# Two chunks at a time in a fused linear-attention and feed-forward kernel

## The chip, the cores and the metric

The kernel runs on one core of one Trainium2 chip. The metric is the device time of one execution in microseconds (us), as the median of several runs. The engines are TensorE (PE; PEld is its weight load), VectorE (DVE), ScalarE (ACT), GpSimd (POOL) and SyncE (SP), which here issues almost all DMAs.

## The reference

For 4 batches, 8 heads, 768 time steps and head size 48, a decayed linear attention is computed, and its output goes through a feed-forward block with a softmax-weighted unit and a layer norm:

```python
for t in range(S):
    kt, vt, rt = (k[:, :, t], v[:, :, t], r[:, :, t])
    cur = np.einsum('bhd,bhe->bhde', u[None] * kt, vt)
    y[:, :, t] = np.einsum('bhd,bhde->bhe', rt, state + cur)
    state = w[None, :, :, None] * state + np.einsum('bhd,bhe->bhde', kt, vt)
# x: y as (3072, 384)
h = x @ w_in                                   # (3072, 1024)
e = np.exp(h - h_max)
solu = h * (e / (np.sum(e, axis=-1, keepdims=True) + 1e-09))
ln = (solu - mu) / np.sqrt(var + 1e-06) * g_ln # mu, var over the 1024
out = ln @ w_out                               # (3072, 384)
```

All arithmetic is in float32; the weights arrive as 64-bit words.

## The kernel before

The time axis is cut into 6 chunks of 128 steps, so there are N = 24 units (batch, chunk), ordered chunk by chunk with the four batches next to each other. A first path, `direct_path`, computes everything under the assumption that decays, weights and sums lie in a safe range, and writes a flag `bad`; a general path (not executed in these runs) would follow if the flag were set.

Per unit i these helpers issue the work:

- `load` brings k, r and v of a unit (three DMAs on SP). `decay_k` and `decay_r` (GpSimd, L674 and L681) multiply k and r with decay tables; `weigh` (GpSimd, L687, L688) and `sum_own` (VectorE, L692) form the diagonal of the scores, and `diagonal` (ScalarE, L698, eight instructions) writes it into AT.
- k and r are transposed. For units below FIRST = 9 that is done on TensorE (`turn_r`, `turn_k`, L710 and L718). For later ones `halve_rk` splits the 32-bit words into 16-bit halves (ScalarE L859, VectorE L860), a transposing DMA turns them (SP, L834), and `join_rk` puts the words together again (VectorE, L839).
- `scores` (TensorE, L733) multiplies k and r into a PSUM tile of two banks; VectorE copies the lower triangle into AT (L735).
- `finish` multiplies state and AT with r and v into y_ps (TensorE, L760), copies it into xT (ScalarE, L772), forms the outer product kv_ps (TensorE, L778) and updates the state (VectorE L784, GpSimd L785).
- `ffn_in` is the first matmul (TensorE, L795, into h_ps, the only buffer of two banks) and the exponential with its sum (ScalarE, L798). `unit` is the reciprocal and the product (VectorE, L805, L807) and the centring and squares (ScalarE, L809, L810); `deviation` (GpSimd) makes the scale of the layer norm. `halve_ln` (ScalarE, L845), a transposing DMA and `join_ln` (VectorE, L839) turn the result into lnT.
- `ffn_out` is the second matmul (TensorE, L877, o_ps), its scaled copy (ScalarE, L879) and the store (SP, L880).

The order of every engine's instructions is written out by hand: the loop over i issues helper after helper, and every engine takes its instructions strictly in that order. At stage i the loop works on unit i+3 (decays), i+2 (joins, diagonal), i+1 (scores), i (heads and state), j = i - LA = i - 2 (first matmul) and l = i - LA - LO = i - 7 (second matmul). So TensorE's order of a steady stage is h_ps, o_ps, at, y_ps, kv_ps. PSUM tiles tr_ps, tk_ps, y_ps, kv_ps and o_ps rotate through the four one-bank buffers of psM.

The weights are also checked. Each of the 14 weight pieces is loaded a second time, one at each stage from i = 12 on (L506); at the next stage `check_words` takes magnitudes and their sum (ScalarE, L558) and the least (VectorE, L560). `check_range` at i = 10 checks the decays from a row loaded for it, and `check_sums`, ahead of the last `ffn_out`, joins all checks through a small matmul n_ps into `bad`.

## Time and profile before

| | us |
|---|---|
| Median of 6 runs (354.76 to 355.03) | 355.0 |
| The profiled execution | 354.66 |
| Its span, first to last instruction | 352.8 |
| TensorE busy in the span | 337.0 |
| ScalarE busy | 242.4 |
| VectorE busy | 210.7 |
| GpSimd busy | 176.8 |

The span is the time between the first and the last instruction of the profiled execution; the rest of its time lies around it. A busy share is an average over stages, so what a change is worth is read from the stage that it touches: from the chain of work that ended last, which names at each step what released it, and from the timeline. Matmul records of different array tiles overlap, so the distance between their starts tells more than the duration of one.

### The profile page before, as it was taken

Reading aid. Unit: us, or ns where it says so; the run is one execution under the profiler, and the core shown is the slowest. Engines: PE = TensorE matmul, PEld = TensorE weight load, DVE = VectorE, ACT = ScalarE, POOL = GpSimd, SP = SyncE. Lnnn points to the kernel's source line nnn. Section 1 sums busy time; section 2 is a strip of 40 time slices with the busy share of each in tenths; the row PEclk is TensorE's granted clock in tenths of the full one; section 3 lists DMA queues with packets and bytes.
Section 4 is the critical chain, followed back from the end, with each engine's and each line's share of the span. In section 5 each row is a group of like instructions: output and inputs, shape, how many; then the busy total and the mean of one; then the engine's idle time right before and its main releaser. Section 6 shows DMA issues by size and latency. Waiting matters only on the chain.

```text
span 352.8 us, 8407 instructions
## 1 busy us (share of the span) xinstructions
PE 337.0 (96%) x3427; PEld 203.6 (58%) x3427; DVE 210.7 (60%) x323; ACT 242.4 (69%) x457; POOL 176.8 (50%) x196
## 2 busy tenths in 40 slices
PE   2699999999999999999999999999999999999993
PEld 2475566656566566556566566565565565545563
DVE  7795888786468567665865765765772441323320
ACT  3775888988897668677767778778687464465510
POOL 3889667784865754944945846746730000000000
PEclk9999999999999999999999999999999999999999
DMA  8999996269999768988887978966663523541641
GB/s 170 264 236 232 234 219 84 56 106 157 191 195 158 146 130 154 208 173 168 188 167 170 195 162 177 195 151 119 150 129 62 126 69 59 128 124 46 143 103 36
DMA packets 164878, 52.75 MB, mean 150 GB/s; under 512 B 157917, under 2 KB 161246, under 8 KB 164830
## 3 DMA queue, kind: packets, MB, share of 16 engines
q1 hardware_dynamic: 164686, 51.92, 71.9%
q8 instruction: 29, 0.48, 0.6%
q10 hardware_dynamic: 144, 0.20, 0.2%
q14 instruction: 19, 0.16, 0.1%
HBM read 26.94 MB, written 4.72 MB: 90 GB/s over the span
## 4 chain that ended last, share of the span: by engine, by line
PE 89%; POOL 3%; issue 2%; ACT 2%; DVE 1%; DMA 1%; SPq 0%; POOLq 0%
PE o_ps L877 35%; PE h_ps L795 35%; PE y_ps L760 10%; PE at L733 6%; PE kv_ps L778 2%; ACT AT L698 1%; DMA g_sb<-in_moe_g_ln_dram 1%; PE tk_ps L718 1%; POOL kp L674 1%; POOL rku L687 1%; PE tr_ps L710 0%; POOL vt L581 0%; POOL rku L688 0%; DVE solu L807 0%; POOL w_in_sb L540 0%
## 5 line engine op out<-in xcount | busy, mean ns | idle before, releaser
L795 PE MATMUL h_ps<-w_in_sb,xT 128*128 128x512 f32 x288 | 129.9, 600 | 0.6 <-DVE solu L807 0.5
L877 PE MATMUL o_ps<-w_out_sb,lnT 128*128 128x384 f32 (+1 forms) x400 | 127.3, 473 | 0.0
L877 PEld LDWEIGHTS o_ps<-w_out_sb,lnT 128*128 128x128 f32 x400 | 75.1, 190 | 52.8 <-issue 9.1
L795 PEld LDWEIGHTS h_ps<-w_in_sb,xT 128*128 128x128 f32 x288 | 52.8, 190 | 60.5 <-issue 58.0
L698 ACT ACTIVATE AT<-ident,own 128x128 f32<-128x128 f32 x192 | 58.6, 390 | 6.0 <-DVE own L692 6.0
L785 POOL TENSOR_TENSOR state<-state,pw 64x192 f32<-64x192 f32 x32 | 25.6, 801 | 63.0 <-DVE state L784 61.6
L735 DVE COPY_PREDICATED AT<-later,at 128x1024 f32<-128x1024 uint32 x24 | 31.9, 1328 | 31.4 <-PE at L733 31.4
L845 ACT COPY halves<-solu 128x2048 uint16<-128x2048 uint16 x24 | 45.4, 1893 | 0.0
L839 DVE COPY lnT<-halves 128x2048 uint16<-128x2048 uint16 x24 | 37.5, 1563 | 11.7 <-DMA halves<-halves 11.7
L809 ACT ACTIVATE solu<-solu,st 128x1024 f32<-128x1024 f32 x24 | 27.5, 1148 | 22.6 <-DVE solu L807 22.6
L798 ACT ACTIVATE e<-h_ps 128x1024 f32<-128x1024 f32 x24 | 24.5, 1022 | 18.2 <-PE h_ps L795 18.2
L816 POOL TENSOR_SCALAR st<-st 128x1 f32<-128x1 f32 x24 | 7.1, 294 | 59.2 <-ACT e L810 59.2
L674 POOL TENSOR_TENSOR kp<-kpad,kdec 128x512 f32<-128x512 f32 x24 | 31.6, 1319 | 7.5 <-ACT kdec L621 6.4
L807 DVE SCALAR_TENSOR_TENSOR solu<-h_ps,st,e 128x1024 f32<-128x1024 f32 x24 | 30.8, 1284 | 2.5 <-DVE st L805 0.5
L688 POOL TENSOR_TENSOR rku<-rku,rpad 128x384 f32<-128x384 f32 x23 | 28.9, 1256 | 1.8
L839 DVE COPY rk<-halves 128x2048 uint16<-128x2048 uint16 x15 | 21.5, 1433 | 11.4 <-DMA halves<-halves 11.1
L733 PE MATMUL at<-rk 48*64 48x128 f32 (+1 forms) x768 | 27.9, 265 | 0.1
L733 PEld LDWEIGHTS at<-rk 48*64 48x64 f32 x768 | 21.8, 139 | 10.5 <-issue 8.6
L681 POOL TENSOR_TENSOR rp<-rpad,rdec 128x512 f32<-128x512 f32 x15 | 27.5, 1832 | 0.0
L760 PE MATMUL y_ps<-AT,vt 128*32 128x128 f32 x768 | 26.1, 275 | 0.7 <-issue 0.7
L860 DVE COPY halves<-rp 128x1024 uint16<-128x1024 uint16 x15 | 19.8, 1318 | 11.3 <-POOL rp L681 11.3
L810 ACT ACTIVATE e<-solu 128x1024 f32<-128x1024 f32 x24 | 25.4, 1057 | 0.8
(82 smaller groups left out, 319.1 us busy)
## 6 DMA issues: line engine op xcount, KB each, us to landing
raw<-in_moe_w_in_dram SPq DMA_DIRECT2D x12, 512.0 KB, 5.7
raw<-in_moe_w_out_dram SPq DMA_DIRECT2D x16, 384.0 KB, 4.3
kpad<-in_k_dram SPq DMA_DIRECT2D x24, 192.0 KB, 4.3
rpad<-in_r_dram SPq DMA_DIRECT2D x24, 192.0 KB, 5.1
vt<-in_v_dram SPq DMA_DIRECT2D x24, 192.0 KB, 4.6
out_dram<-o SPq DMA_DIRECT2D x23, 192.0 KB, 2.2
halves<-halves SPq DMA_TRANSPOSE x39, 4.5
u_bc<-in_u_dram ACTq DMA_DIRECT2D x1, 192.0 KB, 3.4
```

Source lines behind the costliest of these rows:

```text
L674: nc.gpsimd.tensor_mul(X["kp"].rearrange("p h d -> p (h d)"), kpads[i % NLD].rearrange("p h d -> p (h d)"), kdec.rearrange("p a d -> p (a ...
L681: nc.gpsimd.tensor_mul(X["rp"].rearrange("p h d -> p (h d)"), rpads[i % NLD].rearrange("p h d -> p (h d)"), rdec.rearrange("p a d -> p (a ...
L688: engine.tensor_mul(rku, rku, rpads[i % NLD][:, :, 0:D])
L698: nc.scalar.activation(out=AT[:, h, :], in_=ident, func=ACT.Copy, scale=X["own"][:, h])
L733: nc.tensor.matmul(pss[ts(c, P), q, a, c * P :], X["kT"][rows, a, ts(c, P)], X["rT"][rows, a, c * P :], start=True, stop=True)
L735: nc.vector.copy_predicated(A4, later.unsqueeze(1).to_broadcast([128, 2, HP, T]), pss)
L760: nc.tensor.matmul(y_ps[32 * g : 32 * g + 32, j, :], lhsT, rhs, start=(g not in opened), stop=stop, skip_group_check=True)
L795: nc.tensor.matmul(h_ps[:, ts(n, NX)], X["xT"][:, j, :], w_in_sb[:, j, ts(n, NX)], start=(j == 0), stop=(j == KD - 1))
L807: nc.vector.scalar_tensor_tensor(out=solu, in0=X["h"], scalar=rs, in1=X["e"], op0=ALU.mult, op1=ALU.mult, accum_out=tot)
L839: nc.vector.tensor_copy(out=words.bitcast(U16).rearrange("p n (t o) -> p o n t", o=2), in_=turned)
L845: nc.scalar.copy(out=both.rearrange("p (o n) -> p o n", o=2), in_=split(X["solu"]))
L877: nc.tensor.matmul(o_ps, X["lnT"][:, f, :], w_out_sb[:, f, part], start=(f == 0), stop=(f == KF - 1))
```

## The change

From i = 7 on, the loop takes two units at a time. On TensorE the order of a pair is `ffn_in(j)`, `ffn_out(l)`, `ffn_in(j+1)`, `ffn_out(l+1)`, then the scores of two units, then the heads of two units, then one `outer` for both (one kv_ps tile with a half for each). `finish` is cut into `heads`, `take_y`, `outer` and `update`, and the copy of the scores becomes `take_scores`.

The scores now have four one-bank PSUM tiles in place of one of two banks, two of them for odd units from i = 9 on; `turn_r`, `turn_k` and a table use these two earlier in the run. psM has two buffers in place of four. The copy of the scores is two instructions, one for each bank.

On ScalarE and VectorE, exponential and `unit` stand ahead of the transposing helpers of their half of the pair; `join_ln(l+2)` stands at the end of a pair, so that lnT is ready for the next. The weight checks go one a pair from i = 7 on, through a buffer of their own (one for the loaded words), and at the end of the last pairs another is added to have all 14 done before `check_sums`. `check_range` and its load are gone: the decays are copied from the transposed tile at the start and compared in `check_sums`.

```diff
-    psM = ctx.enter_context(tc.tile_pool(name="psM", bufs=4, space=PSUM))
+    psM = ctx.enter_context(tc.tile_pool(name="psM", bufs=2, space=PSUM))
...
-    pss = psA.tile([128, 2, HP, T], F32, name="at")
-    nc.vector.memset(pss, 0.0)
+    pss = [psA.tile([128, HP, T], F32, name=f"at{n}") for n in range(4)]
+    for ps in pss[:2]:
+        nc.vector.memset(ps, 0.0)
...
+    nc.vector.tensor_copy(out=decays, in_=wd_ps)
...
-        X["kp"] = apool.tile([128, H, P], F32, name="kp", bufs=4)
+        X["kp"] = apool.tile([128, H, P], F32, name="kp", bufs=5)
...
-        nc.vector.copy_predicated(A4, later.unsqueeze(1).to_broadcast([128, 2, HP, T]), pss)
+        X["scores"] = ps
+
+    def take_scores(i):
+        A4 = live[i]["AT"].rearrange("p (a q) t -> p q a t", q=2)
+        for q in range(2):
+            nc.vector.copy_predicated(A4[:, :, q, :], later.to_broadcast([128, HP, T]),
+                                      live[i]["scores"][q])
...
+    def outer(chunks):
+        chunks = [i for i in chunks if i < N and units[i][1] < C - 1]
+        if not chunks:
+            return
+        kv_ps = psM.tile([128, 2, HP, D], F32, tag="m", name="kv_ps")
+        for n, i in enumerate(chunks):
+            X, vt = live[i], vts[i % NV]
+            X["kv"] = kv_ps[:, n]
...
+    checks, checked = list(range(len(pieces))), []
+    def check_next():
+        for p in checked:
+            check_words(p)
+        checked[:] = [checks.pop(0)] if checks else []
+        for p in checked:
+            load_weights(p, "check", 1)
+
+    sum_own(FIRST)
+    for i in range(LA + LO, N + LA + LO, 2):
+        j, l = i - LA, i - LA - LO
+        for n in (i, i + 1):
+            if n + 5 < N:
+                load(n + 5, "kr")
+            if n + 3 < N:
+                load(n + 3, "v")
+        new = [n for n in (i + 1, i + 2) if FIRST <= n < N]
+        late = i == LA + LO
+        if late:
+            ffn_in(j)
+            unit(j)
+        for n in (i + 3, i + 4):
+            if n < N:
+                decay_k(n)
+                decay_r(n)
+                weigh(n, nc.gpsimd)
+        for n in (j - 2, j - 1):
+            if LO - 1 <= n < N:
+                deviation(n)
+        if l + 2 < N:
+            halve_ln(l + 2)
+        for n in new[:1]:
+            diagonal(n)
+        join_ln(l + 1)
+        for n in new[:1]:
+            join_rk(n)
+        if j < N and not late:
+            ffn_in(j)
+            unit(j)
+        if i + 3 < N:
+            halve_rk(i + 3)
+        for n in new[1:]:
+            join_rk(n)
+        check_next()
+        ffn_out(l)
+        if l + 3 < N:
+            halve_ln(l + 3)
+        if j + 1 < N:
+            ffn_in(j + 1)
+        for n in new[1:]:
+            diagonal(n)
+        if j + 1 < N:
+            unit(j + 1)
+        if l + 1 == N - 1:
+            check_sums()
+        ffn_out(l + 1)
+        if i + 4 < N:
+            halve_rk(i + 4)
+        for n in (i + 3, i + 4):
+            if n < N:
+                sum_own(n)
+        now = [n for n in (i + 1, i + 2) if n < N]
+        for n in now:
+            scores(n)
+        for n in now:
+            take_scores(n)
+        now = [n for n in (i, i + 1) if n < N]
+        for n in now:
+            heads(n)
+            take_y(n)
+        outer(now)
+        for n in now:
+            update(n)
+        if l + 2 < N:
+            join_ln(l + 2)
+        if i >= N - 1:
+            check_next()
```

## The prediction

> **What bounds the kernel now.** I began with the busy table and the 40 slices of the page, then followed the chain that ended last, then the timeline of one steady stage and of the tail, and last the waits and the DMA table.

> ```profile
> PE 337.0 (96%) x3427; PEld 203.6 (58%) x3427; DVE 210.7 (60%) x323; ACT 242.4 (69%) x457; POOL 176.8 (50%) x196
> PE   2699999999999999999999999999999999999993
> PE 89%; POOL 3%; issue 2%; ACT 2%; DVE 1%; DMA 1%; SPq 0%; POOLq 0%
> ```

> TensorE is busy from the third slice on, and 89% of the chain is its own work. The other engines are at 50 to 69%: making them faster gains nothing, making them late can cost. The chain in order of time shows a stage and then the tail:

> ```profile
> 199.92 5.16 PE o_ps L877 x16
> 205.08 1.02 PE at L733 x24
> 206.10 1.67 PE y_ps L760 x56
> 207.77 0.34 PE kv_ps L778 x32
> 208.11 5.35 PE h_ps L795 x12
> 213.46 5.16 PE o_ps L877 x16
> ...
> 305.81 5.16 PE o_ps L877 x16
> 310.97 5.15 PE h_ps L795 x12
> 316.12 25.80 PE o_ps L877 x80
> 341.92 0.12 PE n_ps L658 x2
> 342.04 5.41 PE o_ps L877 x32
> ```

> A stage is 5.35 + 5.16 + 1.02 + 1.67 + 0.34 = 13.54 us with no hole: only the length of TensorE's own pieces can be gained. The same 12 matmuls of h_ps take 5.35 after kv_ps and 5.15 after o_ps. So 0.20 of a stage is not matmul work but the change of shape before it. The timeline of TensorE alone says the same of the small pieces:

> ```profile
> 205.72 0.39 PE L733 MATMUL at<-rk 48*64 48x128 f32 x4
> 206.03 0.86 PE L760 MATMUL y_ps<-rk,state 128*32 128x128 f32 x24
> 206.71 1.06 PE L760 MATMUL y_ps<-AT,vt 128*32 128x128 f32 x32
> 207.58 0.52 PE L778 MATMUL kv_ps<-vt,kp 128*32 128x48 f32 x32
> ```

> The 32 records of the second y row are 8 rows of four that run side by side, and they start in 207.58 - 206.71 = 0.87 us: 0.109 a row. 14 rows (56 records) are 1.53, not 1.67. The last four score records span 0.39 at about 0.27 each, so the 128-column ones start some 0.11 apart; 8 of them are 0.87, not 1.02. From y to kv, both 128*32, nothing is lost.

> **What pairing saves.** In a pair TensorE runs h, o, h, o, scores twice, heads twice, kv once for both. Against two old stages the second h follows o (5.35 to 5.15: 0.20), the second scores follow scores (1.02 to 0.87: 0.15), the second heads follow heads (1.67 to 1.53: 0.14); kv is 2 x 0.34 either way. That is 0.49 a pair, 27.08 to 26.59. Whole pairs are those with i = 7, 9 ... 21: eight. At i = 23 the order h, o, h, o, y only moves one h from after y to after o and another the other way: nothing. So 8 x 0.49 = 3.9 us. The h part (1.6) is shown by two rows of the chain; the rest (2.3) I work out from start times, between 0 and 2.3. I take 2.3, because y to kv shows that pieces of one tile shape follow at full pitch.

> **Does a wait take its place?** I walk one pair with rows of the trace, from the start of h(j) at 0: h(j) to 5.35, o(l) to 10.51, h(j+1) to 15.66, o(l+1) to 20.82, scores to 22.71, heads to 25.91, kv to 26.59.
> - h_ps is one buffer, and h(j+1) now follows one o later (5.16) instead of o, scores, heads and kv (8.19). Exp (about 1.2 with its accumulator), reciprocal and unit's product (1.28) must lie in 5.16. In a tail stage free of other work h ends near 305.8 and the product at 308.5: 2.7. VectorE has ahead of it: four state adds (2 x 0.74, from 0.1), two join_ln (1.56 each by the group's mean) and one join_rk (1.43), so it is free near 6.2, and Exp ends near 6.75. Product at 8.3, slack 2.2. The transposes of these joins were issued in the pair before.
> - ScalarE in the first half: halve_ln 1.89 and eight diagonals 2.45 from -0.1, done at 4.3, ahead of Exp at 5.55; then unit (2.33), the kp half (1.05), one word check (0.73), o, halve_ln, done at 15.0 before Exp(j+1) at 15.9. Second half: diagonals to 19.5, unit to 21.9, o(l+1) to 22.4, kp half to 23.4, xT(i) 24.4 to 24.9.
> - psM has two buffers, not four, for o, o, y, y, kv in turn. heads(i) takes o(l)'s (free at 13), heads(i+1) that of o(l+1), free at 22.4, needed at 24.4; kv takes y(i)'s, free at 24.9, needed at 25.9, the thinnest cover (0.9). If ScalarE were 1 us late, y(i) itself would set that copy, so the cover holds.
> - heads(i+1) needs take_scores(i+1) of the same pair: scores(i+1) end at 21.85, two copies of about 0.69 (bound: the 128x512 products L711 take 0.69) end at 23.3, and AT is read from 25.0. Slack 1.7.
> - GpSimd: two chunks of kp, rp, rku (1.32 + 1.83 + 1.10 + 1.26 each), four state products (0.80), deviations: 16 of 26.6; rp(i+3) is there at about 7.5, before VectorE wants it.
> - SP: six loads, four transposes, one check load, two stores a pair, in order. The check load waits for ScalarE's word check; behind it wait o's store and the next transposes, whose data ScalarE writes later anyway. One check load a pair instead of two is less DMA.
> So steady stalls are 0. The first pair (i = 7) has Exp and unit ahead of halve_ln and the diagonals, which leaves o(1)'s copy at 24.5, needed at 24.4: 0 to 0.4, I take 0.2.

> **The start.** The extra copy of decays costs about 0.09 (the pitch of its neighbours) in the table chain that GpSimd's kp waits for; the split memset and take_scores about 0.05 each (2 x 0.69 against 1.33), mostly covered, since VectorE idles 40% of the span; without the cover, 9 x 0.05. Together 0.1, bounds 0 to 0.5. The wrow check (four instructions, 2.1 us of VectorE and a load) goes; VectorE has idle time, so 0.

> [...]

> **The tail pays.** Before, the last word check was at i = 26, long before check_sums. Now 14 pieces go one a call through one buffer: piece 13 is loaded only after the check of piece 12, which ScalarE does after o(21), and check_sums needs it before n_ps, which stands on TensorE ahead of the last ffn_out. Before shows each step:

> ```profile
> 311.06 0.58 ACT L879 ACTIVATE o<-o_ps,st 128x384 f32<-128x384 f32 x1
> 311.54 0.54 ACT L558 ACTIVATE mag<-raw 128x384 f32<-128x384 f32 x1
> 312.07 0.42 SPq L506 DMA_DIRECT2D raw<-in_moe_w_out_dram  x1
> 312.20 0.55 DVE L560 TENSOR_REDUCE least<-mag 128x1 f32<-128x384 f32 x1 [3.64 <-ACT mag L558]
> ```

> From the end of o(21) on TensorE: o's copy starts at 0.18, mag at 0.66, its release at 1.32, the load's issue at 1.35. The page has 4.3 as median landing of this load; in the quiet end the DMA view of three single windows has 2.9, 3.0 and 3.4. With 3.0 it lands at 4.35, mag's release is at 5.06, least ends at 5.64, six small compares (pitch 0.08, as at 339.83) and the reduce (0.23) end near 6.5, n_ps starts at 6.6. TensorE is done with o(22) at 5.16: a stall of 1.4, bounds 1.1 (2.9, tight) to 2.7 (4.3).

> The first transposes after TensorE's early idle time are slow (four in 1.12 us at 15.77, 0.66 at 21.88), though the clock row reads 9 throughout. [...]

> **Sum.** The profiled execution took 354.66 (span 352.8, 1.9 around it), 0.34 under the median of 355.0. -3.9 + 1.4 + 0.2 + 0.1 = -2.2: 352.5 against it, 352.8 against the median. Own range: full saving, stall 1.1 and nothing else, 352.2; half of the 2.3, stall 2.0, start 0.4, first pair 0.3, 354.9.

> **Rivals.**
> 1. Only h gains: the second scores and heads still pay. -1.6 + 1.7 = +0.1, 355.1. For it: no row shows two scores in succession. Against: y to kv. 0.12.
> 2. Slower, by one mechanism: h_ps's shorter window. If VectorE's joins wait for a transpose, unit's product passes 10.51 and TensorE stands still in every pair. It decides when the product ends over 5.16 after h. For it: the waits list has 11.1 us in 4 waits of rk for halves (mean 2.8, longest 4.7). 2.8 after 6.2 minus the slack is about 0.8 a pair, 8 x 0.8 = 6.4: 359.2. Against: the joins now stand a half pair or more behind their transposes. 0.10.
> 3. The tail stall is far larger: the load lands after 5.7, the median of the w_in pieces, which makes 4.1 of 1.4 and 355.5 of the sum. Against: little else moves by then. 0.05.
> Forecast 0.73.

> Under 0.2% (0.7 us) a measurement of this kernel hardly tells from no change. Faster by more: 0.71 (the forecast less its upper end); same: 0.14 (that end and rival 1); slower: 0.15 (rivals 2 and 3). The range 351.7 to 355.6 leaves out rival 2, what lies above rival 3's price, and a little below.

> **What would show it.** In the chain: every second h_ps at 5.15, two scores in about 1.89, two heads in 3.20; n_ps late by 1 to 2 us behind VectorE's least; no TensorE idle time behind L826's product or behind xT. A pair near 26.6 is right; 27.1 is rival 1; 28 or more with h_ps waiting for solu is rival 2.

## The result

The changed kernel took 355.55 us (median of 17 runs, 354.38 to 356.88) beside 355.02 of the kernel before (38 runs): a ratio of 1.0015, 95% interval 1.0007 to 1.0023. Run once more, unaltered, on another chip it took 355.17 (11 runs) beside 354.93: 1.0003, 0.9994 to 1.0012. So it gains nothing; if anything it is slightly slower. 352.8 was forecast.

Its profiled execution took 354.64 us, the span was 352.9 (before 354.66 and 352.8). The busy row and the chain's shares of the page after:

```profile
PE 334.0 (95%) x3427; PEld 204.6 (58%) x3427; DVE 210.4 (60%) x347; ACT 240.8 (68%) x457; POOL 178.7 (51%) x196
PE 78%; ACT 10%; issue 3%; DVE 3%; POOL 2%; DMA 2%; SPq 0%; POOLq 0%; ACTq 0%; DVEq 0%
```

TensorE works 3.0 us less (337.0 before) for the same 3427 matmuls: the saving is there. The span did not fall with it, so TensorE stands still longer. Its share of the chain fell from 89 to 78%, which is not as much idle time: from 59.7 to 98.4 us the chain runs through ScalarE and VectorE while TensorE works too, and ends in one wait of 0.78. Below, h(n) and o(n) are the matmuls of `ffn_in` and `ffn_out` of unit n, heads(n) those into y_ps, kv(n) those into kv_ps, xT(n) ScalarE's copy of y_ps, Exp(n) the exponential and unit(n) the work of `unit`. The chain of waits shows a steady pair, start and length in us:

```profile
180.55 5.35 PE h_ps L814 x12
...
191.06 5.15 PE h_ps L814 x12
...
201.37 1.89 PE at L728 x48
203.26 3.19 PE y_ps L761 x112
206.46 0.68 PE kv_ps L791 x64
```

No hole (the two o left out are 5.16 each), and 26.59 from h to h. The first pair is another matter. TensorE's timeline, then ScalarE's, each with start, length and, in brackets, the idle time before it and what ended it:

```profile
98.38 0.86 PE L761 MATMUL y_ps<-rk,state 128*32 128x128 f32 x24 [0.78 <-ACT o L898]
```

```profile
80.49 1.01 ACT L817 ACTIVATE e<-h_ps 128x1024 f32<-128x1024 f32 x1
...
95.52 1.15 ACT L828 ACTIVATE solu<-solu,st 128x1024 f32<-128x1024 f32 x1 [1.63 <-DVE solu L826]
...
97.76 0.56 ACT L898 ACTIVATE o<-o_ps,st 128x384 f32<-128x384 f32 x1
```

heads(8) needs the PSUM buffer of o(1), and ScalarE copies o(1) only at 97.76, after unit(6), in which it waited 1.63 for VectorE's product. The first line, Exp(5), is where its lateness begins (see below). The tail, from the chain and then ScalarE's timeline:

```profile
306.72 1.71 PE y_ps L761 x56
308.45 0.49 ACT xT L777
...
308.98 5.42 PE h_ps L814 x12
314.40 25.81 PE o_ps L896 x80
...
340.25 0.55 DVE least L562
...
341.69 0.19 PE n_ps L654 x2
```

```profile
339.58 0.55 ACT L560 ACTIVATE mag<-raw 128x384 f32<-128x384 f32 x1 [3.35 <-DMA raw<-in_moe_w_out_dram]
```

There are two holes: 0.60 between heads(23) and h(23), which waits for the copy xT(23), and 1.49 ahead of n_ps, behind the last piece's load, mag and least.

The two chains can be laid side by side at common marks. h(7), at 99.83 before, starts at 100.79: +0.96, of which 0.05 is the start and 0.91 the first pair. From there seven pairs take 185.11 instead of 188.46: -3.35. The rest, to TensorE's end at 347.29 (before 347.45), is 2.23 longer. Together -0.16, and behind TensorE's end 0.2 is lost, so that the two spans come out alike.

### The profile page after: what moved, and what is told of

Its sections match the earlier page's. It is cut to its first block, busy times and chain, and to the rows that moved or that the text cites. A ratio compares the mean times of both kernels' runs of the same rounds, so it can differ in the third digit from the quotient of the medians.

```text
span 352.9 us, 8478 instructions
## 1 busy us (share of the span) xinstructions
PE 334.0 (95%) x3427; PEld 204.6 (58%) x3427; DVE 210.4 (60%) x347; ACT 240.8 (68%) x457; POOL 178.7 (51%) x196
## 4 chain that ended last, share of the span: by engine, by line
PE 78%; ACT 10%; issue 3%; DVE 3%; POOL 2%; DMA 2%; SPq 0%; POOLq 0%; ACTq 0%; DVEq 0%
PE o_ps L896 32%; PE h_ps L814 30%; PE y_ps L761 9%; PE at L728 5%; ACT AT L693 3%; ACT halves L864 2%; DVE solu L826 2%; PE kv_ps L791 1%; ACT solu L828 1%; ACT e L817 1%; DMA g_sb<-in_moe_g_ln_dram 1%; POOL kp L669 1%; DMA wq<-in_w_dram 1%; ACT e L829 1%; PE at L713 1%
## 5 line engine op out<-in xcount | busy, mean ns | idle before, releaser
L804 POOL TENSOR_TENSOR state<-state,pw 64x192 f32<-64x192 f32 x32 | 29.4, 919 | 68.9 <-DVE state L803 67.1
L669 POOL TENSOR_TENSOR kp<-kpad,kdec 128x512 f32<-128x512 f32 x24 | 42.5, 1771 | 6.9 <-ACT kdec L623 6.4
L817 ACT ACTIVATE e<-h_ps 128x1024 f32<-128x1024 f32 x24 | 24.5, 1020 | 28.9 <-PE h_ps L814 28.8
L735 DVE COPY_PREDICATED AT<-later,at 128x512 f32<-128x512 uint32 x48 | 31.6, 730 | 14.9 <-PE at L728 14.9
L824 DVE RECIPROCAL st<-sums 128x1 f32<-128x1 f32 x24 | 3.9, 164 | 60.0 <-ACT e L817 59.7
L858 DVE COPY lnT<-halves 128x2048 uint16<-128x2048 uint16 x24 | 33.8, 1443 | 3.1 <-DMA halves<-halves 2.9
L826 DVE SCALAR_TENSOR_TENSOR solu<-h_ps,st,e 128x1024 f32<-128x1024 f32 x24 | 30.8, 1284 | 2.1
L777 ACT COPY xT<-y_ps 128x384 f32<-128x384 f32 x24 | 11.5, 478 | 24.1 <-PE y_ps L761 24.1
L858 DVE COPY rk<-halves 128x2048 uint16<-128x2048 uint16 x15 | 27.5, 1835 | 0.0
L683 POOL TENSOR_TENSOR rku<-rku,rpad 128x384 f32<-128x384 f32 x23 | 26.3, 1145 | 1.8
L728 PE MATMUL at<-rk 48*64 48x128 f32 (+1 forms) x768 | 26.2, 266 | 0.0
```

The lines of the kernel that those rows point to most:

```text
L669: nc.gpsimd.tensor_mul(X["kp"].rearrange("p h d -> p (h d)"), kpads[i % NLD].rearrange("p h d -> p (h d)"), kdec.rearrange("p a d -> p (a ...
L728: nc.tensor.matmul(ps[q][ts(c, P), a, c * P :], X["kT"][rows, a, ts(c, P)], X["rT"][rows, a, c * P :], start=True, stop=True)
L735: nc.vector.copy_predicated(A4[:, :, q, :], later.to_broadcast([128, HP, T]), live[i]["scores"][q])
L804: nc.gpsimd.tensor_mul(S, S, wT)
L826: nc.vector.scalar_tensor_tensor(out=solu, in0=X["h"], scalar=rs, in1=X["e"], op0=ALU.mult, op1=ALU.mult, accum_out=tot)
L858: nc.vector.tensor_copy(out=words.bitcast(U16).rearrange("p n (t o) -> p o n t", o=2), in_=turned)
```

## The experiments

Three theories of where the 3.35 went, one for each hole, were each tried alone and then all at once, on one chip, beside the kernel before (354.95, 29 runs).

**The last check a pair earlier.** An additional check_next() at i = 13 loads and checks the last piece earlier.

```
-        if i >= N - 1:
+        if i >= N - 1 or i == 13:
             check_next()
```

> The word checks are one call ahead (an extra one in the pair with i = 13, where ScalarE and VectorE have room), so the last is done before ffn_out(22) ends. Theory A (the gain of pairing is given back in three places: the first pair about 1.2 us, h(23) behind xT(23) about 0.6, n_ps behind the last word check about 1.5): n_ps follows o_ps without idle time, the profiled span falls by 1.4 to 1.6, and, since the stall hangs on when a DMA lands, the runs spread less than the 2.5 us of the changed kernel; median 353.5 to 354.1, ratio to before 0.996 to 0.9975. Theory B (the stall is not what ends the run: the store and the end of ScalarE would come as late without it): no change, 355.5.

Measured: 354.09 us (12 runs), ratio to before 0.9981 (0.9964 to 0.9997). The hole is gone from the chain:

```profile
315.50 25.80 PE o_ps L896 x80
341.30 0.12 PE n_ps L654 x2
```

From the o run to the last one it is 25.91 instead of 27.48, so 1.57 of the tail is this wait. The rest of theory A was not met: the profiled span fell by 0.2 only (352.9 to 352.7), since this trace loses 1.0 in two stops inside kv, of which more below, starts h(1) 0.1 later and has 0.3 more behind TensorE's end; and the runs spread as widely as those of the changed kernel (353.49 to 356.31).

**halve_ln before unit in the first pair.** ScalarE does a piece of its work ahead of a wait of 1.63 for VectorE's product, instead of behind it.

```
         if late:
             ffn_in(j)
+            halve_ln(l + 2)
             unit(j)
...
-        if l + 2 < N:
+        if l + 2 < N and not late:
             halve_ln(l + 2)
```

> In the first pair alone, halve_ln(l + 2) goes on ScalarE between the exponential and unit, into the 1.6 us in which ScalarE waits for VectorE's product. Theory A: o(1)'s copy comes 1.6 us earlier, heads(8) does not wait for it, the first pair is 0.9 to 1.0 shorter, the rest as in the changed kernel; median 354.6 (354.3 to 354.9). Theory B (the first pair waits for the two psM buffers whatever ScalarE's order): no change, 355.5.

Measured: 354.97 us (12 runs), 0.9993 (0.9977 to 1.0009). In the chain of its first pair both heads and kv run through:

```profile
96.74 3.19 PE y_ps L761 x112
99.94 0.68 PE kv_ps L791 x64
```

From o(0) to the next pair's h it takes 21.51 instead of 22.49: 0.98, in the trace. The median lies 0.58 under the changed kernel's, just above the range of theory A, and the intervals of the two ratios overlap, so it is the trace that shows the hole gone. This trace has h(1) 0.8 later (37.25, 36.44) and two stops in kv as well.

**The last heads before the last o.** At i = 23 heads and take_y stand ahead of ffn_out(l + 1), as an old stage had them.

```
+        if i == N - 1:
+            heads(i)
+            take_y(i)
         ffn_out(l + 1)
...
-        now = [n for n in (i, i + 1) if n < N]
+        now = [n for n in (i, i + 1) if n < N and i < N - 1]
```

> At i = 23, heads(23) and its copy stand ahead of the second ffn_out instead of after it, so h(23) does not follow at once. Theory A: the 0.55 us of waiting for xT(23) goes, o after y costs no more than h after y; median 355.0 (354.8 to 355.2). Theory B: the wait moves to o(17), whose psM buffer is freed by ScalarE, no change, 355.5.

Measured: 355.24 us (12 runs), 1.0013 (0.9995 to 1.0031): by the median alone unclear, 0.3 under the changed kernel and just above the range of theory A. The chain settles it; o now covers the copy of xT(23), and h follows o at 5.15:

```profile
302.86 1.67 PE y_ps L761 x56
304.52 5.36 PE o_ps L896 x16
309.88 5.15 PE h_ps L814 x12
```

From the scores before to the long o run it is 32.92 instead of 33.59: 0.67.

**All three.**

> All three edits. Theory A: they add, 1.5 + 0.95 + 0.55 = 3.0 off the changed kernel, median 352.5 (352.2 to 353.0), ratio to before 0.993, and the steady saving of 0.48 a pair stands in the total. Theory B (part of the loss lies in runs that the profile does not show, at the start): 353.5 or more, or the spread stays.

Measured: 353.04 us (6 runs), 0.9944 (0.9925 to 0.9964), and on another chip once more 352.50 (6 runs), 0.9935 (0.9916 to 0.9954). That beats both kernels, though the first is at the edge of theory A's range. The three holes of 1.57, 0.98 and 0.67 are the greater part of what ate the gain: 3.2 in the traces, and about 2.5 by the ratios to before (1.0015 to 0.9944, 1.0003 to 0.9935). What is missing is partly a fourth hole, which the chain of the 353.04 kernel shows inside kv(16):

```profile
205.67 0.50 PE kv_ps L791 x44
206.16 0.11 issue
206.27 0.45 PE kv_ps L791 x19
```

"issue" is time in which TensorE waited for nothing that the profile shows. kv takes 1.05 instead of 0.68 (h starts at 206.72). Inside a kv, matmuls start 11 ns apart on average and at most 23; here one step is 316 ns, after the 44th, and one of 240 in kv(10), after the 42nd. The three traces above have such steps too, of 318 to 521 ns, always after the 42nd matmul of kv(10) or the 44th of kv(16). The pairs that hold them last 26.9 to 27.2.

**Is it the saving that was thought?** Scores and heads take turns again inside a pair, all else as changed.

```
         now = [n for n in (i, i + 1) if n < N]
         for n in now:
+            if n + 1 < N:
+                scores(n + 1)
+                take_scores(n + 1)
             heads(n)
             take_y(n)
```

> The changed kernel, but in every pair the scores and heads stand as before: scores(i+1), heads(i), scores(i+2), heads(i+1), then kv for both; h, o, h, o and everything else stay. Theory (the saving is the change of tile shape that TensorE no longer makes): the second scores cost 1.02 again and the second heads 1.67, +0.15 +0.14 = +0.29 a pair, a steady pair of 26.87 instead of 26.58, eight pairs +2.3: about 357.8 against the 355.55 of the changed kernel. Rival (the saving comes from one kv for two chunks or from a wait that is gone): pair 26.58, 355.5.

Measured: 356.97 us (5 runs), 1.0048 (1.0035 to 1.0061), 1.8 over the changed kernel on the same chip, where 2.3 was worked out. kv starts at 154.14, 181.01, 207.88 and 234.75: 26.87 a pair, as worked out. In TensorE's timeline the second scores again take 1.02 to the start of the next line:

```profile
178.44 1.09 PE L728 MATMUL at<-rk 48*64 48x128 f32 x32
179.46 0.86 PE L761 MATMUL y_ps<-rk,state 128*32 128x128 f32 x24
```

So 0.29 a pair hangs on this order alone, to 0.01 us, and the one kv for two units is out as its cause. That it is the change of tile shape, and not something else that changes between scores and heads, is read from the other seams: y to kv and h to o share a shape, differ in operands and PSUM tile, and lose nothing, while o behind y takes 5.36 (in the experiment on the last heads) and behind h 5.16.

**The changed kernel again.**

> The changed kernel, unaltered, once more, for a second trace beside the experiments. Its first trace lost nothing in kv, but four experiments' traces show TensorE standing still 0.1 to 0.6 us inside kv(10) near 127 us and kv(16) near 207 us, with nothing awaited. Theory (the two heads and kv run through 224 short matmuls in 5.8 us and the next 16 KB of TensorE's instructions come too late in some runs): the stop is seen here too, at the 42nd to 44th matmul of these kv, 0.3 to 1.0 us in all, with a median near 355.5 and a spread from 354.4 to 357. Rival (the stops belong to the experiments): no stop, and the gap between the trace's 354.6 and the median 355.5 lies at the start or in the last store.

Measured: 355.17 us (11 runs). The theory missed here: none of its seven kv has a step above 23 ns, and neither had the first trace. The stops are shown for traces of the experiments, the one with scores and heads in turn among them (236 ns after the 42nd), not for the changed kernel itself. What made up its distance from trace (354.64, 354.98) to median is not settled.

**What stops inside kv?** The page's table of queues has one that brings instructions:

```profile
q8 instruction: 29, 0.48, 0.6%
```

That is 29 packets of 16 KB. TensorE issues 6927 instructions in the trace, two for each matmul, and from 124.4 to 204.4 us seven packets go by beside some 1800 of them: about 256 a packet. Two scores, two heads and kv put 240 matmuls (64, 112 and 64) in a row into 5.8 us. The theory: if a block of 256 runs out before the next has come, TensorE stops, and at a fixed instruction. Three kernels move the ends of the blocks with transposes of the identity, whose output nothing reads, in TensorE's idle time before 12.7 us.

```
+    def pad(n):
+        for _ in range(n):
+            nc.tensor.transpose(pss[3][:, 0, :], ident, ident)
+
     wd_ps = psM.tile([128, HP], F32, tag="m", name="wd_ps")
+    pad(10)
     nc.tensor.transpose(wd_ps, wq.rearrange("a q d -> a (q d)"), ident[0:HP, 0:HP])
...
+            pad(7)
             turn_r(0)
```

> The kernel with all three repairs (353.04, stops of 0.3 and 0.4 inside kv(10) and kv(16) in its trace) with 17 more transposes of the identity, whose output nothing reads, while TensorE is idle before 6.6 us. They move every later instruction of TensorE back by 34 places. Theory (a block of 256 instructions, fetched in about 3.1 to 3.4 us from the start of the one before, ends at kv's 42nd matmul): the ends now fall at kv's 25th and at the 2nd or 3rd matmul of the next h, where the block before lasts 3.2 to 3.3 us: no stop or less than 0.2 in all, about 352.5. Rival (the stops come from data, from PSUM or from traffic of the DMA engines at that time): the stops stay at the 42nd matmul, 353.0.

> As the one with 17, but 32 more transposes in TensorE's idle time before 12.7 us, so 64 places. Theory of the blocks: the ends fall at kv's 10th matmul near 126 and 206 us, where nothing stops, and at about kv's 52nd matmul in other pairs, near 100 and 180 us, where the block before lasts 2.7 us: stops of 0.3 to 0.7 there, none at 126 and 206, about 353.3. Rival: stops at the 42nd matmul near 126 and 206 as in the kernel with the repairs alone, 353.0. If the transposes are not wholly hidden, the start is later by up to 0.5 in both.

The second has pad(11) and pad(10) at these places, and 5 and 6 more around turn_r(1).

Measured, with 17: 353.68 us (6 runs), 0.9964 (0.9948 to 0.9979). No step in any kv, as the theory had it; a stop in the h behind the first pair's kv, after its 3rd matmul, the place that was named. But it is 1.17 long, where less than 0.2 was expected. The chain behind three matmuls of that h:

```profile
101.40 1.17 issue
102.57 4.02 PE h_ps L819 x9
```

With 32: 356.41 us (12 runs), 1.0034 (1.0014 to 1.0053). The stops come after kv's 53rd matmul near 99 us and its 55th near 183 (named: the 52nd near 100 and 180), and the large ones at 126 and 206 are gone; one of 0.1 is left in kv(16) near 210, after the 13th (named: the 10th, none). TensorE's timeline, then the windows (width, busy time of PE, PEld, DVE, ACT and POOL, granted clock, DMA share, GB/s):

```profile
98.19 0.77 PE L796 MATMUL kv_ps<-vt,kp 128*32 128x48 f32 x53
101.71 0.36 PE L796 MATMUL kv_ps<-vt,kp 128*32 128x48 f32 x11 [2.75 <-issue]
```

```profile
99.00:101.70 2.70, 0.00 (x0) 0.00 (x0) 0.00 (x0) 0.00 (x0) 0.00 (x0) 1.00 1.28 155
103.00:106.40 3.40, 3.40 (x6) 1.31 (x5) 3.34 (x5) 3.20 (x9) 3.17 (x4) 0.50 0.96 175
```

The one near 183 is 0.46, within 0.3 to 0.7; the one near 99 is 2.75. So the places follow the count of instructions, and data, PSUM and a fixed time are out as causes. The traces hold the count itself: numbered from 0 over TensorE's matmuls, weight loads and sequencer instructions, the first one after a stop is 2497, 3009, 4289 or 4801 in all 14 stops of over 0.1 us (eight traces, with and without transposes), 193 more than a multiple of 256 each time. And each of the 14 ends 1.3 to 1.6 us after the end of an instruction packet. In the two traces of the changed kernel the same packets had ended 1.2 to 1.6 us before TensorE reached 3009 and 4801: it did not stop, but had next to nothing to spare.

The sizes were wrong in the first pair, where the DMA engines are fuller than in later ones (share 1.28 against 0.96 in the window from 204 to 208 of the changed kernel). The packet there took 1.1 us, no longer than others, but began at 99.18, when TensorE had already stopped: 3.1 us after the block before had begun (2.6 with 17), against 0.2 to 1.2 at the stops of later pairs. What kept it is not settled.

**Ten transposes, beside none.**

The h that the next passage calls h(8) is h(7), the one with the stop of 1.17.

> The kernel with all three repairs and 10 more transposes in TensorE's idle time, so 20 places. With 17 the stops in kv were gone, but one of 1.17 us came inside h(8) of the first pair, where the traffic is densest and a block took about 5.4 us. Theory of the blocks: the ends fall at kv's 32nd matmul near 126 and 206 us, where the block before lasts 3.1 us, and at about the 10th matmul of h(8) near 103 us, where it lasts 6.7: stops of 0 to 0.3 at the first two places, none in h(8), about 352.7. Rival (any extra work at the start costs, or the stops fall by chance): 353.5 or more, stops elsewhere than near these matmuls.

> The kernel with all three repairs, once more, as the neighbour of the one with 10 transposes on the same chip. Theory: stops of 0.2 to 0.5 at kv's 42nd and 44th matmul near 126 and 206 us, the first pair without any, 353.0 (352.8 to 353.9). Rival: no stops, 352.5.

Measured: 353.06 us (6 runs), 0.9939 (0.9919 to 0.9958), and 352.50 for the neighbour without transposes, the second figure above. In the traces both came as the theory had them: with 10, no kv step above 60 ns and no stop in h(7); without, steps of 427 and 247 ns after the 42nd and 44th. The time did not follow: with 10 h(1) starts 0.5 later (37.12, 36.59) and n_ps waits 0.61, because check_sums came behind a join_ln that waited 1.8 for its transposes. The stops are explained; that taking them away pays is not shown.

## Why the prediction was wrong

- **The steady saving was right.** 26.59 a pair, second h at 5.15, two scores 1.89, two heads 3.19. Rival 1 is out, and the interleaved kernel shows the 0.29 by itself.
- **Steady stalls 0: right.** In the changed kernel's two traces no pair after the first and before i = 23 has a hole, so rival 2 is out (its price was also a slip: 2.8 less the slack of 2.2 is 0.6 a pair, not 0.8); VectorE's product ended 8.1 us after h's start (8.3 worked out).
- **First pair, "0 to 0.4, I take 0.2": this term failed.** The pair should have won 0.49 and lost 0.2; it lost 0.91. heads(8) came 0.97 late. ScalarE was taken as on time at the start of the pair, but Exp(5), in this trace at 80.49, comes some 2.2 after o(0) has started and h(5) has ended, since ScalarE still works off rk, halve_ln, the kp half, xT and the eight diagonals of the loop before; the old trace has the same lag (80.38), where it cost nothing. ScalarE also waits 1.63 at unit for VectorE, twice in this pair. o(0) itself waits 0.14 for xT(6) and takes 5.43.
- **"At i = 23 the order ... only moves one h ...: nothing": this step failed.** The lengths cancel, but a dependence was overlooked: heads(23) gives y, ScalarE copies xT(23), and h(23) reads it at once, with no o between. 0.60 of hole, 0.67 in all by the experiment. So the sign "no TensorE idle time behind xT" did not hold.
- **n_ps, 1.4: right** (1.49). The load landed 3.2 after its issue, against the 3.0 taken. Rival 3 is out.
- **Start, 0.1: 0.05 in the trace**, which says little beside the spread of h(1) below. In take_scores the view is `p (a q) t -> p a q t`, so that `[:, :, q, :]` takes the heads of one bank. Split, it is 2 x 730 ns instead of 1328, 0.13 each and not 0.05; the chain that ended last names this copy nowhere, so it cost nothing that shows.
- **Against the median.** The sum was set off by 0.34 from trace to median. That distance is 0.9 for the first trace of the changed kernel and 0.2 for the second. The twelve traces show what varies from run to run: h(1) starts between 35.7 and 37.4, and TensorE's end to the span's end takes 5.4 to 6.4. The sum of two errors, 1.2 in the first pair and 0.7 at i = 23, is 1.9 of the 2.7 by which the median was missed; n_ps (1.57 for 1.4) and the time behind TensorE's end add 0.2 each, and the rest lies in this spread.

## What to carry to other kernels

Grouping work of one tile shape on TensorE paid here what the change of shape costs, 0.49 of 27.08 us a pair, and it could be read off the chain beforehand. The gain was lost at the seams, 0.98 us in the first pair, 0.67 and 1.57 in the last: for the first and the last round of a new order, walk every operand's producer again, with the lag of each engine as the trace has it there and not as in the steady round. A last check or sum in front of the last matmul should have its load out a round early.
